# A delta-rule recurrence feeding a soft mixture of experts: keys taken ahead, norms on GpSimd, output products in pairs

## The chip, the cores and the metric

One core of a Trainium2 chip runs the whole program in one launch. The metric is the device time of one execution in microseconds (us). The core has five instruction streams: TensorE (PE in the profile) multiplies matrices out of the on-chip memory SBUF into the accumulator banks PSUM; VectorE (DVE) and ScalarE (ACT) work element by element and empty PSUM; GpSimd (POOL) works element by element on SBUF and issues some transfers; SyncE (SP) only issues transfers (DMAs).

## The reference

For each of 4 batches and 8 heads a state of 48 x 48 is carried over 768 steps:

```python
k_n = k / (np.linalg.norm(k, axis=-1, keepdims=True) + 1e-06)
for t in range(S):
    y[:, :, t] = np.einsum('bhd,bhde->bhe', q[:, :, t], state)
    v_old = np.einsum('bhde,bhd->bhe', state, kt)
    state = state + bt[..., None] * np.einsum('bhd,bhe->bhde', kt, vt - v_old)
```

The outputs y, laid out as 3072 rows of 384, are the x of a soft mixture of 8 experts with 4 slots each:

```python
logits = x @ phi
d = softmax over rows of logits;  slot_input = d.T @ x
slot_out[e] = np.maximum(slot_input[e] @ w1[e], 0.0) @ w2[e]     # 384 -> 1024 -> 384
c = softmax over slots of logits; result = c @ slot_out
```

Everything is float32.

## The kernel before

**Chunks and groups.** The 768 steps are cut into 12 chunks of 64 (`n`), and two chunks make a group (`g`, 6 of them). Inside a chunk the recurrence is turned into matrix products, for which a triangular system has to be inverted. The inversion is done for a whole group at once on VectorE.

**Loads.** `load_kv` loads a chunk of keys or values in two halves of three DMAs each, `load_q` a chunk of queries in two halves of one DMA each. Nearly all are issued by SP. `beta` is loaded by 16 small DMAs on GpSimd's queue. The identity matrix, needed by every transposition, is built on GpSimd (`ident`).

**Key and query products.** `turn(n, a, j)` transposes keys (`trk`, a = 0) or queries (`trq`, a = 1) on PE and copies them out of PSUM (`evTk`, `evTq`). `gram(n, j, part)` multiplies a chunk's keys with its keys (part 0, `...k`), its keys with its queries (part 1, `...q`), or both in one product of twice the width. The key part is copied out by ACT (`evP`, `evR` for the inversion, `evB`), the query part is masked on VectorE (`mskA`). Before the change only group 0 has the two parts apart.

**Inversion** (`invert(g)`). `spread` transposes blocks of the key products on VectorE; it needs the `evP` and `evR` copies of both chunks. From the diagonal, the squared lengths of the keys, the norms and factors are made (`ssq`, then `ln` and `sq` on ACT, then `rec`, `quo`, `nrm`, `nsq`, `inv`, `gm` on VectorE), each on a tile of 128 x 32. `nT` transposes the norms for the scaling of the values (`vs`, on GpSimd from group 1 on). `diag` and `scale` prepare the system. Then come 31 pairs `col`/`sub` (15 for group 0, which is halved and put together on PE by `z`, `v` and `mrg`), each pair depending on the one before. `back` transposes back; behind it `tw` (ACT, and GpSimd for one half from group 1 on) and `j` with `evJ` finish the group on TensorE and ACT.

**Step** (`step(n)`). Chunk after chunk: `ks` (keys by state) and `r` (values less that, VectorE), `tr` with `evW`, `fix` with `evU`, `s` with `evS` (the new state), `qs` (queries by state) and the part `au`, which is mixed into the next chunk's `tr`. `try`, `lg`, `trd`, `trL`, `sl`, `trE` with their copies and the VectorE steps `max`, `emx`, `esb`, `esm`, `enr`, `acc` are the routing of two chunks into the slots.

**Experts and output.** `first` (`fst`), `turnh` (`trh`), `second` (`snd`) are the experts; their weights are loaded into places of the SBUF that earlier stages have left free, and into places of the first weights once those are used. `put(d)` sums the halves (`sum`, `so`) and makes the output products `om`, which ACT and VectorE copy (`evo`) and SP or GpSimd store (`st`).

**Order.** The kernel lists its operations and then emits them in the order of a written-out string (`ORDER`), a permutation of that list; each engine runs its own operations in that order, one after the other. `BANKS` gives the PSUM bank of each product, and `GATES` holds a load of expert weights back until a given product has run. A planner outside the kernel, with fixed costs per operation, made the three strings.

Of the kernel before, what the change touches and what calls it, by code (L numbers as in the profile page):

```python
# [12 lines left out]
ALU = mybir.AluOpType  # L13
# [1 line left out]
PSUM = bass.MemoryType.PSUM  # L15

ORDER = (
    "#*##%x#,#&#0#+#3#$#2#-#%#)#'#(#E#G#D#=#F#6#>$K#?#7#4#8#.#C#@$d#A#O#<#B#H#P#9$e#:#V#I$C#;$G$D#/#Q$H$E"
    "#R$g#U$|#J$F%y#S#N$I#K#L$J#M#T#5#W&Q$r$h$s$i#X$L#Y#Z#[#]#^#d#_$f%z#`&0$?#a#b%{#c$;$@#e#f$A#g$<$M#h#i"
    "$N#j$Y#k&1#l#m#n$t$Z#o$=#p$u$B'}$v#q$>#r$j#s$w$O#t$z&l#u$P#v#1${$k$[#w$x#x$l&P$y#y$]#z&2$Q$p#{$^#|$R"  # L20
    "&3&R$m#}$S'~$q$b$_#~$`$#$$$T$c$W&k$%$a$X$n&S$&&T$o$'$U$V&_&U$}&`$)$($~$-'%$*%#%$%%%&%'%(%-%)(#%*$+%,"
    "$.%+%.%/%0%1%2%3%4$/%5$,%6$2%7%8$1%9%:%;%<%=%>%?$3$0%@$7&#%A$5%B$6%C%|%D&$$4&y%E(Q&%$8%F%}%~%G&z%H&&"
    "$9%I(R$:&a%J&'&V%K&b&*%L&W&c%M&+(s%N&,(t&X%O&g%P&d&(%Q&]%R&Y&o&)&^&e)0&-(S%S&f&4)/%T&.&h&j&/%U&Z%V&["
    "%W&p&9&5&i%X&6&:%Y%Z&;&7*A%[&8%]%^%_%`&>&H%a&<%b*B&K&?%c&=%d&B&I%e&@%f&C%g%h&w&D%i&m%j&A%k&x%l&E%m&n"
    "($(q&F&q&G(%()%t&u(r&r&{(*&s&t)E%u&v&|*t&}%o%p&~%w'&%v(;%r*u%n&J%q'''$'((&')'*'#'+%s','-'2'.*C'/(w'1"
    "(')%(((x(.+:'0)&'3'4(++9'5'6'7(u'8(9'9(8':)#';(v'<(:)$*v'='>(/)='?(,(2'@(-)3'A(3(0'B)4+Q'C(4(>'D+R(<"
# [99 lines left out]
def kernel(  # L126
# [249 lines left out]
    def invert(g):  # L376
# [5 lines left out]
        def spread():  # L382
# [6 lines left out]
        ACTO("ln%d" % g, 32, lambda: S_.activation(A(n0), A(n0), ACT.Ln), more=20, r=[n0], w=[n0])  # L389
        ACTO("sq%d" % g, 32, lambda: S_.activation(A(n0), A(n0), ACT.Exp, scale=0.5), more=20, r=[n0], w=[n0])  # L390
        DVE("rec%d" % g, 32, lambda: V.reciprocal(A(qq), A(n0)), more=165, r=[n0], w=[qq])
        DVE("quo%d" % g, 32, lambda: V.tensor_tensor(A(qq), dg(lb), A(qq), op=ALU.mult), r=[lb], w=[qq])
        DVE("nrm%d" % g, 32, lambda: V.scalar_tensor_tensor(A(nrm), A(n0), 2e-6, A(qq), op0=ALU.add, op1=ALU.add),
            more=55, r=[n0, qq], w=[nrm])
        DVE("nsq%d" % g, 32, lambda: V.scalar_tensor_tensor(A(gm), A(nrm), 0.25, A(nrm), op0=ALU.mult, op1=ALU.mult),
            more=55, r=[nrm], w=[gm])
        DVE("inv%d" % g, 32, lambda: V.reciprocal(A(gm), A(gm)), more=165, w=[gm])
        DVE("gm%d" % g, 32, lambda: V.tensor_tensor(A(gm), A(cbb)[:, 32 * g:32 * g + 32], A(gm), op=ALU.mult),
            r=[cbb], w=[gm])
        DVE("diag%d" % g, 32, lambda: V.tensor_copy(dg(tt), A(gm)), r=[gm], w=[tt])  # L400

        def blk(t):
# [397 lines left out]
    def mkrd():  # L800
# [1 line left out]
        V.reciprocal(A(sS)[:, 3:4], A(sS)[:, 2:3])  # L802
    DVE("rd", 0, mkrd, more=190, r=[prd], w=[(sS, 2)])

    hrb = [Buf(Yr[0], F), Buf(Yr[0] + F, F)]
    hTb = [Buf(Yr[0] + 2 * F, F), Buf(Yr[0] + 3 * F, F)]
    HF, W2 = F // 2, 2 * Dm
    late = [Vr[0], Vr[1], Sbd[0].addr, Sbd[0].addr + W2, KQr[0], KQr[0] + W2, Kr[0], BBr[1], Vr[2],
            Sbd[1].addr, Sbd[1].addr + W2] + [KQr[0] + W2 * x for x in (2, 3, 4)]
    late += Rr + [Ur[0], TWr[1], TWr[1] + W2, AAr[0], Ur[1], AAr[0] + W2, BBr[2]]  # L810
    late += [w1b[e, kk].addr for e in range(3) for kk in range(NKT)]

    def load_w2(qq):
        for u in range(4):
# [47 lines left out]
    obs = [Buf(w1b[e, kk].addr + Dm * x, Dm) for e in range(3, 7) for kk in range(NKT) for x in H2]  # L862

    def second(qq, u, d):
        def prod():
# [8 lines left out]
    def put(d):  # L874
# [6 lines left out]
        DVE("so%d" % d, HC, lambda: V.tensor_scalar(  # L881
            A(so[d]), F1(p4)[:, 0:HC], A(sS)[:, 3:4], None, op0=ALU.mult), r=[p4, (sS, 2)], w=[so[d]])
        for m in range(NG):
            for j in H2:
                po, ob = pl.ps(), obs.pop(0)

                def om(m=m, j=j, po=po):
                    for c in H2:
                        r = slice(64 * c + 32 * j, 64 * c + 32 * j + 32)
                        for e in H2:  # L890
                            a = HD * e + C * m
                            x = HC * (1 - e)
                            mm(F1(po)[ha(c), x:x + HC], A(cT)[r, a:a + C], A(so[d])[r],  # L893
                               tile_position=(64 * c + 32 * j, 64 * c))
                PE("om%d.%d.%d" % (d, m, j), 500, om, rec=16, r=[cT, so[d]], w=[po])
                (DVE if j else ACTO)("evo%d.%d.%d" % (d, m, j), Dm, lambda po=po, ob=ob, j=j: (  # L896
                    V.tensor_copy if j else S_.copy)(A(ob), F1(po)[:, 0:Dm]), r=[po], w=[ob])
                byp = j and m % 2

                def st(j=j, m=m, ob=ob, byp=byp):  # L900
# [33 lines left out]
```

## Time and profile before

| | |
|---|---|
| median of 3 runs | 312.4 us (310.45 to 313.92) |
| profiled execution | 314.56 us, its span 312.8 us |
| TensorE, VectorE, ScalarE, GpSimd busy | 248.1, 212.5, 172.3, 98.4 us |
| mean granted TensorE clock | 0.896 of full speed |
| moved by DMA | 45.11 MB |

The profile is one execution. PE stands for matmuls, PEld for its weight loads, DVE for VectorE, ACT for ScalarE, POOL for GpSimd, SP for SyncE; an engine with a q behind it is its queue of issues. In a timeline row stand the start and the length in us, the engine, the line, the instruction, its output and input and, in brackets, how long the engine had been idle before it and what ended that. In a group row stand the count, the busy time and the mean length in ns. A row of a stretch gives its ends, its length, the busy time of each engine shown with its count of instructions, the granted clock, the DMA share and GB/s. L179 is the line of the helper for ACT's copies, so it holds most of them.

### The profile page before, as it was taken

The numbers are of one execution on the slowest core, as the hardware profiler recorded it, in microseconds if no ns is written. First come the engines' busy times: TensorE is split into PE (matmuls) and PEld (weight loads), VectorE is DVE, ScalarE is ACT, GpSimd is POOL, SyncE is SP. The second block draws the span as 40 slices with busy tenths as digits, with TensorE's granted clock in tenths as the row PEclk, the third lists the DMA queues.
The fourth block names the chain that finished last, engine by engine and source line by source line (L and its number), as shares of the span: only waits on it lengthen the run. The fifth ranks groups of instructions, "written<-read, shape, count | busy, mean of one in ns | idle before, by whom it ended". The sixth has DMA issues, their size and how long they took to land.

```text
span 312.8 us, 14219 instructions
## 1 busy us (share of the span) xinstructions
PE 248.1 (79%) x6168; PEld 199.2 (64%) x6168; DVE 212.5 (68%) x581; ACT 172.3 (55%) x417; POOL 98.4 (31%) x215
## 2 busy tenths in 40 slices
PE   0746965698899789798975887979879698999990
PEld 0644755697787676687854776777758585247770
DVE  3347868974979889999899998997983145010160
ACT  1453471358687858779874768836458454111340
POOL 9820004305058700594006009854403000000031
PEclk9975675559999999999999998979999799899995
DMA  8997990025655444403963153785899579492477
GB/s 110 130 125 106 133 127 5 6 46 86 106 102 81 76 81 70 82 9 55 109 179 54 36 114 99 239 256 145 290 364 332 195 229 355 175 375 77 153 224 231
DMA packets 90734, 45.11 MB, mean 144 GB/s; under 512 B 78480, under 2 KB 83216, under 8 KB 90672
## 3 DMA queue, kind: packets, MB, share of 16 engines
q1 hardware_dynamic: 87632, 42.53, 59.0%
q0 software_dynamic: 896, 1.28, 1.7%
q8 instruction: 48, 0.79, 1.1%
q10 hardware_dynamic: 2144, 0.39, 1.0%
q14 instruction: 14, 0.11, 0.2%
HBM read 39.47 MB, written 4.72 MB: 141 GB/s over the span
## 4 chain that ended last, share of the span: by engine, by line
PE 53%; DVE 18%; ACT 9%; issue 9%; DMA 4%; SPq 3%; POOL 1%; POOLq 0%; ACTq 0%; DVEq 0%
ACT sb L179 9%; PE pb L347 6%; PE pb L328 5%; PE pb L589 5%; PE pb L572 4%; PE pb L829 4%; PE pb L868 4%; PE pb L560 4%; DVE sb L426 4%; DVE sb L421 3%; PE pb L496 3%; PE pb L893 3%; PE pb L603 3%; PE pb L470 2%; DVE sb L384 2%
## 5 line engine op out<-in xcount | busy, mean ns | idle before, releaser
L179 ACT ACTIVATE sb<-pb 128x384 f32<-128x384 f32 (+5 forms) x252 | 111.3, 465 | 54.6 <-PE pb L328 12.9
L532 POOL TENSOR_SCALAR sb<-sb 128x48 f32<-128x48 f32 x160 | 57.7, 387 | 42.9 <-issue 17.5
L421 DVE TENSOR_TENSOR sb<-sb 128x31 f32<-128x31 f32 (+15 forms) x155 | 53.9, 348 | 4.3
L426 DVE TENSOR_TENSOR sb<-sb 128x31 f32<-128x31 f32 (+15 forms) x155 | 53.2, 343 | 4.3
L179 ACT ACTIVATE sb<-pb,sb 128x256 f32<-128x256 f32 (+1 forms) x96 | 39.9, 451 | 28.9 <-PE pb L347 13.4
L328 PE MATMUL pb<-sb 128*128 128x128 f32 x192 | 33.5, 320 | 20.4 <-DMA sb<-in_k_dram 13.0
L328 PEld LDWEIGHTS pb<-sb 128*128 128x128 f32 x192 | 25.0, 163 | 25.2 <-issue 14.8
L485 POOL TENSOR_SCALAR sb<-sb 128x512 f32<-128x512 f32 x10 | 16.6, 1664 | 66.7 <-DVE sb L448 66.7
L347 PE MATMUL pb<-sb 48*64 48x128 f32 (+1 forms) x896 | 29.8, 280 | 4.4 <-DVE sb L366 2.6
L572 PE MATMUL pb<-sb 64*64 64x48 f32 x768 | 28.9, 228 | 4.3 <-DVE sb L562 1.7
L572 PEld LDWEIGHTS pb<-sb 64*64 64x64 f32 x768 | 26.9, 144 | 6.5 <-DVE sb L562 1.7
L347 PEld LDWEIGHTS pb<-sb 48*64 48x64 f32 x896 | 24.3, 149 | 8.0 <-ACT sb L179 3.1
L516 PE MATMUL pb<-sb 64*64 64x48 f32 x768 | 27.7, 222 | 1.4 <-issue 1.4
L589 PE MATMUL pb<-sb 64*64 64x96 f32 x384 | 23.8, 263 | 4.0 <-issue 2.5
L516 PEld LDWEIGHTS pb<-sb 64*64 64x64 f32 x768 | 25.1, 136 | 1.7 <-issue 1.7
L366 DVE TENSOR_TENSOR sb<-pb,sb 128x512 f32<-128x512 f32 x24 | 16.5, 688 | 12.8 <-ACT sb L179 9.4
L902 POOL DMA_DIRECT2D out_dram<-sb x6 | 4.5, 743 | 64.8 <-DVE sb L896 64.8
L589 PEld LDWEIGHTS pb<-sb 64*64 64x64 f32 x384 | 19.3, 145 | 6.4 <-issue 3.1
L560 PE MATMUL pb<-sb 128*64 128x96 f32 x352 | 20.1, 257 | 1.9 <-ACT sb L179 1.7
L622 PE MATMUL pb<-sb 128*64 128x96 f32 x352 | 18.9, 250 | 1.9 <-ACT sb L179 1.4
L496 PE MATMUL pb<-sb 64*64 64x64 f32 x384 | 15.8, 240 | 5.1 <-issue 2.8
L560 PEld LDWEIGHTS pb<-sb 128*64 128x64 f32 x352 | 15.9, 141 | 6.1 <-ACT sb L179 4.6
(114 smaller groups left out, 334.9 us busy)
## 6 DMA issues: line engine op xcount, KB each, us to landing
sb<-in_moe_w_dram SPq DMA_DIRECT2D x24, 512.0 KB, 5.2
sb<-in_moe_w_dram SPq DMA_DIRECT2D x32, 384.0 KB, 5.4
sb<-in_q_dram SPq DMA_DIRECT2D x24, 192.0 KB, 4.7
out_dram<-sb SPq DMA_DIRECT2D x18, 192.0 KB, 2.5
sb<-in_v_dram SPq DMA_DIRECT2D x24, 96.0 KB, 3.4
sb<-in_v_dram SPq DMA_DIRECT2D x48, 48.0 KB, 3.4
sb<-in_k_dram SPq DMA_DIRECT2D x22, 96.0 KB, 3.9
sb<-in_k_dram SPq DMA_DIRECT2D x44, 48.0 KB, 3.6
```

Source lines behind the costliest of these rows:

```text
L179: S_.activation(o, i, ACT.Copy, **kw)
L328: nc.tensor.transpose(F1(ps)[:, P * h:P * h + P], A(src)[:, x:x + P], ident())
L347: mm(A(ps)[ha(e), i, P * h:P * h + P].rearrange("p (a t) -> p a t", a=2)[:, pr[0]:pr[-1] + 1], x[hd(i), j, h, e], y[hd(i), j, h, e, pr[0]: ...
L421: V.tensor_tensor(p(), v3(tt)[:, j:j + 1, 0:m].broadcast_to(sh), v3(lb)[:, j:j + 1, j + 1:32].rearrange("p x i -> p i x").broadcast_to(sh) ...
L426: V.tensor_tensor(t, t, p(), op=ALU.subtract)
L496: mm(F1(pj)[ha(e), C * h:C * h + C], A(bb)[ha(e), b:b + C], A(lb)[ha(e), b:b + C])
L516: mm(F1(pY[n, j])[ha(1 - e), D * x:D * x + D], A(AA[n])[ha(e), a:a + C], A(UB[n])[ha(e), c:c + D], start=n == 0 and x == 0)
L532: G_.tensor_scalar(y, y, A(nb)[:, c:c + 1], 0.5, op0=ALU.mult, op1=ALU.mult)
L560: mm(bank(pK)[ha(e), j, 2 * D * h:2 * D * h + 2 * D], t4(n, 0)[:, j, 2 * b + h, e], bd()[:, j, b, h, e])
L572: mm(bank(pU[b])[ha(e), j, y:y + D], A(TW[g])[ha(e), a:a + C], A(R)[ha(e), c:c + D], start=x == 4 * b and j == 0)
L589: mm(bank(pU[b])[ha(e), :, y:y + D], A(BBb[g])[ha(e), a:a + C], A(U)[ha(e)].rearrange("p (j x d) -> p x j d", j=2, d=D)[:, x], start=False)
L622: mm(F1(pY[n, j])[ha(1 - e), 2 * D * h:2 * D * h + 2 * D], t4(n, 1)[:, j, h, e], bd()[:, j, h // 2, h % 2, e], start=h == 0)
```

## The change

There are four parts. Group 1 makes its key products apart from its query products, as group 0 does. The keys of chunks 0 to 3 are loaded first, then queries and values; beta's loads now stand ahead of the identity on GpSimd. In groups 1 to 5 the norms and factors are made by GpSimd and ACT (an inverse square root and an inverse from logarithm and exponential, each refined by one step), so VectorE keeps only `nT`, `diag` and `scale` of this part. The two output products of a chunk pair become one operation that writes two PSUM banks. All three strings are new, and with them the order of everything else; places of the expert weights move as well.

```diff
-        DVE("ssq%d" % g, 32, lambda: V.tensor_scalar(A(n0), dg(lb), 1e-30, None, op0=ALU.max), r=[lb], w=[n0])
...
+        if g:
+            t_ = lambda o, x, y: G_.tensor_tensor(A(o), A(x), A(y), op=ALU.mult)
+            lin = lambda o, x, a, b: G_.tensor_scalar(A(o), A(x), a, b, op0=ALU.mult, op1=ALU.add)
+            def root():
+                t_(gm, qq, qq)
+                t_(gm, gm, n0)
+                lin(gm, gm, -0.5, 1.5)
+                t_(qq, qq, gm)
+                t_(nrm, n0, qq)
+                lin(nrm, nrm, 2.0, 2e-6)
+            def inverse():
+                t_(gm, nrm, n0)
+                lin(gm, gm, -2.0, 4.0)
+                t_(n0, n0, gm)
+                t_(n0, n0, n0)
+                G_.tensor_tensor(A(gm), A(cbb)[:, 32 * g:32 * g + 32], A(n0), op=ALU.mult)
+            POOL("ssq%d" % g, 200, lambda: G_.tensor_scalar(A(n0), dg(lb), 1e-30, None, op0=ALU.max), r=[lb], w=[n0])
+            act("ln%d" % g, gm, n0, ACT.Ln, 1.0)
+            act("sq%d" % g, qq, gm, ACT.Exp, -0.5)
+            POOL("root%d" % g, 1000, root, r=[n0], w=[qq, gm, nrm])
+            act("lm%d" % g, gm, nrm, ACT.Ln, 1.0)
+            act("iv%d" % g, n0, gm, ACT.Exp, -1.0)
+            POOL("ivs%d" % g, 850, inverse, r=[nrm, cbb], w=[n0, gm])
+        else:
...
@@ get
-                if g:
+                if g > 1:
                     turn(n, 1, j)
                     gram(n, j)
                 else:
                     gram(n, j, 0)
         invert(g)
-        for n in H2 if not g else ():
+        for n in (2 * g, 2 * g + 1) if g < 2 else ():
@@ expert weights
-    late += [w1b[e, kk].addr for e in range(3) for kk in range(NKT)]
+    late += [w1b[e, kk].addr for e in range(2) for kk in range(NKT)][:32 - len(late)]
@@ put
+            po = pl.ps(2)
+            def om(m=m, po=po):
+                for e in H2:
+                    a = HD * e + C * m
+                    x = HC * (1 - e)
+                    for j in H2:
+                        for c in H2:
+                            r = slice(64 * c + 32 * j, 64 * c + 32 * j + 32)
+                            mm(A(po)[ha(c), j, x:x + HC], A(cT)[r, a:a + C], A(so[d])[r], tile_position=(64 * c + 32 * j, 64 * c))
+            PE("om%d.%d" % (d, m), 830, om, rec=32, r=[cT, so[d]], w=[(po, 0), (po, 1)])
             for j in H2:
-                po, ob = pl.ps(), obs.pop(0)
-       ...
-                PE("om%d.%d.%d" % (d, m, j), 500, om, rec=16, r=[cT, so[d]], w=[po])
+                ob = obs.pop(0)
```

The strings, read as sequences, at the places that the prediction speaks of:

```
SP before:   v0.0 k0.0 q1.1 k1.0 q1.0 k2.0 q0.0 k3.0 k3.1 q3.1 v0.1 q0.1 k4.1 k2.1 ...
SP after:    phi k0.0 k2.0 k1.0 k2.1 k3.0 k3.1 q0.0 q0.1 q1.0 q1.1 v0.0 v0.1 v1.0 v1.1 q2.0 ...
             (k0.1 and k1.1 by ACT's queue in both)
POOL after:  beta ident maskA zeroS0 zeroS1 zeroT0 zeroT1 ssq1 root1 vs2 ivs1 zeroT2 vs3 tw3.1 tw2.1
             zeroT3 ssq2 root2 ivs2 vs4 vs5 tw5.1 zeroT4 tw4.1 ssq3 root3 ivs3 vs6 ...
PE before:   ... trk5.1 trk5.0 s1.1 ks2.0 gram5.0 ks2.1 gram5.1 j3 j2 ...
PE after:    ... ks1.0 s0.1 tr1.0 qs1.0 fix1.0 j2 s1.0 ks1.1 j3 qs1.1 trk5.1 tr1.1 trk5.0 trq6.0
             fix1.1 try0.1 trq6.1 s1.1 gram5.1 gram5.0 ks2.1 ks2.0 ...
DVE before:  ... backT1 r2.0 r2.1 mskA5.0 spread2 ssq2 mskA5.1 rec2 quo2 nrm2 nsq2 nT2 inv2 gm2 scale2 diag2 col2.0
DVE after:   ... col1.27 r1.0 sub1.27 mskA4.1 ... backT1 r1.1 mskA5.1 mskA5.0 spread2 r2.1 r2.0 nT2 scale2 diag2 col2.0
ACT after:   ... evTk2.0 evB3.0 evP3.0 evR3.0.0 evR3.0.1 evP2.1 evTq0.1 evTq0.0 ln0 evTq1.1 sq0 ...
```

More of the change, by code (lines that the diff above doesn't have):

```diff
@@ L60 @@
+    "1$2G1L2F1L1L"
 )
@@ L387, in invert @@
         v3 = lambda t: A(t).rearrange("p (r c) -> p r c", c=32)
-        DVE("ssq%d" % g, 32, lambda: V.tensor_scalar(A(n0), dg(lb), 1e-30, None, op0=ALU.max), r=[lb], w=[n0])
[L389 to L399, printed above, removed]
+        if g:
[14 more added lines that the diff above has]
+                G_.tensor_tensor(A(gm), A(cbb)[:, 32 * g:32 * g + 32], A(n0), op=ALU.mult)
+            act = lambda name, o, x, f, c: ACTO(name, 32, lambda: S_.activation(A(o), A(x), f, scale=c), more=20, r=[x], w=[o])
+            POOL("ssq%d" % g, 200, lambda: G_.tensor_scalar(A(n0), dg(lb), 1e-30, None, op0=ALU.max), r=[lb], w=[n0])
[6 more added lines that the diff above has]
+        else:
+            DVE("ssq%d" % g, 32, lambda: V.tensor_scalar(A(n0), dg(lb), 1e-30, None, op0=ALU.max), r=[lb], w=[n0])
+            ACTO("ln%d" % g, 32, lambda: S_.activation(A(n0), A(n0), ACT.Ln), more=20, r=[n0], w=[n0])
+            ACTO("sq%d" % g, 32, lambda: S_.activation(A(n0), A(n0), ACT.Exp, scale=0.5), more=20, r=[n0], w=[n0])
+            DVE("rec%d" % g, 32, lambda: V.reciprocal(A(qq), A(n0)), more=165, r=[n0], w=[qq])
+            DVE("quo%d" % g, 32, lambda: V.tensor_tensor(A(qq), dg(lb), A(qq), op=ALU.mult), r=[lb], w=[qq])
+            DVE("nrm%d" % g, 32, lambda: V.scalar_tensor_tensor(A(nrm), A(n0), 2e-6, A(qq), op0=ALU.add, op1=ALU.add),
+                more=55, r=[n0, qq], w=[nrm])
+            DVE("nsq%d" % g, 32, lambda: V.scalar_tensor_tensor(A(gm), A(nrm), 0.25, A(nrm), op0=ALU.mult, op1=ALU.mult),
+                more=55, r=[nrm], w=[gm])
+            DVE("inv%d" % g, 32, lambda: V.reciprocal(A(gm), A(gm)), more=165, w=[gm])
+            DVE("gm%d" % g, 32, lambda: V.tensor_tensor(A(gm), A(cbb)[:, 32 * g:32 * g + 32], A(gm), op=ALU.mult),
+                r=[cbb], w=[gm])
@@ L861 @@
     so = [Buf(rt[0] + HC * x, HC) for x in H2]
-    obs = [Buf(w1b[e, kk].addr + Dm * x, Dm) for e in range(3, 7) for kk in range(NKT) for x in H2]
+    obs = [Buf(w1b[e, kk].addr + Dm * x, Dm) for e, kk in [(7, 0), (7, 1), (3, 2)] + [(e, kk) for e in (4, 5, 6) for kk in range(NKT)]
+           for x in H2]
     def second(qq, u, d):
```

95 lines of the change are left out of this document (43 added, 52 removed).

## The prediction

> **What bounds the kernel now.** I read the page's chain first, then the stretches between landmarks on VectorE (DVE), whose order is fixed by the written-out list. The chain's shares:
>
> ```profile
> PE 53%; DVE 18%; ACT 9%; issue 9%; DMA 4%; SPq 3%; POOL 1%; POOLq 0%; ACTq 0%; DVEq 0%
> ```
>
> The chain keeps stepping onto TensorE (PE), yet the middle is paced by DVE. The next view gives each stretch, its length, DVE's busy time with count, TensorE's granted clock, DMA share and GB/s. I cut it at starts of DVE operations: `rec0` 25.09, `col0.0` 28.76, `backT0` 44.22, `col1.0` 53.62, `backT1` 85.38, `col2.0` 96.98, `backT2` 126.06, `col3.0` 134.21, `backT5` 232.25, and the copy `evslb` 265.49, after which the experts start.
>
> ```profile
> 25.09:28.76 3.67, 3.39 (x12) 0.50 0.77 123
> 28.76:44.22 15.46, 11.73 (x39) 0.72 0.91 119
> 44.22:53.62 9.40, 8.63 (x14) 0.50 0.38 45
> 53.62:85.38 31.76, 23.78 (x69) 0.74 0.37 58
> 85.38:96.98 11.60, 9.28 (x16) 1.00 0.52 93
> 96.98:126.06 29.08, 25.72 (x77) 1.00 0.50 78
> 126.06:134.21 8.15, 7.91 (x15) 1.00 0.45 77
> 134.21:232.25 98.04, 89.27 (x250) 0.97 0.57 146
> 232.25:265.49 33.24, 13.03 (x47) 0.94 0.81 282
> ```
>
> From 96.98 to 232.25 DVE is busy 122.9 of 135.3 us: there its own work sets the pace. Before that it also waits (23.78 of 31.76), mostly in one place:
>
> ```profile
> 74.68 0.70 DVE L366 TENSOR_TENSOR sb<-pb,sb 128x512 f32<-128x512 f32 x1 [6.06 <-ACT sb L179]
> ```
>
> After 232.25 DVE is idle most of the time, and PE finishes chunks 10 and 11, routing, experts and output. So I follow DVE to `backT5`, then add the two tail stretches.
>
> **Start: keys ahead.** A chunk of q, k or v is 0.39 MB. Landings in before:
>
> ```profile
> 12.84 1.06 PE L328 MATMUL pb<-sb 128*128 128x128 f32 x8 [0.22 <-DMA sb<-in_k_dram]
> ...
> 26.58 1.94 PE L328 MATMUL pb<-sb 128*128 128x128 f32 x8 [2.53 <-DMA sb<-in_q_dram]
> ```
>
> Counting issues ahead of each, 1.28 MB had landed at the first and 2.95 MB at the second: 122 KB/us. In the new order keys 0 to 3 with phi and beta are 1.72 MB, estimated at 16.4 us; q0 at 19.7, q1 at 22.9. `gram1.1k` now stands behind `trk3.0`, so it runs at about 17.5, and `spread0` starts near 20 (19.5 before). ScalarE (ACT) then holds `ln0` behind the copy of q0 and `sq0` behind one of q1 (22.9, a transposition and two copies): `rec0` at about 25, as before. I take no gain; with 125 KB/us and no landing lag it is 3 us, and 1.5 us of loss if ACT's queue drains late. Beta's 16 issues (8.9 us, row below) now precede the identity, so first transposes start near 10.8; the wait for chunk 3's keys covers that.
>
> Behind `rec0`: `mskA0.0` and `mskA1.1` move ahead of `col0.0`, 0.62 us each (0.70 in the row of L366, and starts overlap by 0.08): `col0.0` at 30.0. The next stretch loses some 3.0 us of waits and two masks and gains `mskA1.0` 0.62, `spread1` 1.85 and `nT1` 0.13: 13.85, `backT0` at 43.85. Then `spread1` (1.8), group 1's norm (1.9) and its ACT wait (0.6) are gone and `mskA2.1` is added: 5.8 instead of 9.4. `col1.0` starts at **49.7** (53.6). This needs `ivs1` by 48; POOL runs it behind `vs2`, which ends near 46. Cover gone, each microsecond costs one.
>
> **Norms off DVE.** Seven small instructions per group leave DVE in groups 1 to 5. What they cost now, from reciprocal to the scaling behind them:
>
> ```profile
> 93.90 0.36 DVE L391 RECIPROCAL sb<-sb 128x32 f32<-128x32 f32 x1
> ...
> 95.62 1.23 DVE L411 TENSOR_TENSOR sb<-sb 128x1024 f32<-128x1024 f32 x1
> ```
>
> That is 1.7 us, 8.5 in five groups if nothing waits. In exchange POOL gets 12 instructions (`ssq` 1, `root` 6, `ivs` 5) and ACT two more. No POOL row shows 32-element arithmetic. The nearest:
>
> ```profile
> L532 POOL TENSOR_SCALAR sb<-sb 128x48 f32<-128x48 f32 x160 | 57.7, 387 | 42.9 <-issue 17.5 <-PE pb L328 13.2 <-DMA sb<-in_v_dram 7.6
> L485 POOL TENSOR_SCALAR sb<-sb 128x512 f32<-128x512 f32 x10 | 16.6, 1664 | 66.7 <-DVE sb L448 66.7
> L271 POOL DMA_DIRECT2D sb<-in_beta_dram x16 | 8.9, 566 | 0.6 <-DMA sb<-in_beta_dram 0.5
> ...
> L282 POOL TENSOR_SCALAR_AFFINE_SELECT sb<-sb 32x64 f32<-32x64 f32 x8 | 1.9, 232 | 0.4
> ```
>
> 387 ns is the upper end, 232 the lower row; an unrowed two-input form could go below, say 0.17, or above. I take 0.3: 3.6 us, plus 1.1 for four ACT steps and hand-overs, 4.7 us of chain. The Trainium skill, GPSIMD Engine Reference, section "Performance versus the Vector engine", speaks against the move: two-input elementwise work takes GpSimd about twice DVE's time. No run here shows such an instruction; twice DVE's 0.2 us would make the chain some 1.2 us longer than I take.
>
> The chain is hidden where `spread` stands well ahead of `back`: group 1, and nearly groups 4 and 5 (4.9 and 4.5 us of DVE work against a chain of some 5 to 5.5; 0.7 and 0.5 us show). In groups 2 and 3 `spread` stands behind `backT`, and DVE waits.
>
> **Group 1 to 2: a new wait.** `mrg0` moves to behind `col1.15`, 63 us. So `tr0.0` starts near 65 (62 before). PE here runs at half clock:
>
> ```profile
> 45.00:69.00 24.00, 17.48 (x657) 16.23 (x658) 21.69 (x52) 8.73 (x21) 6.76 (x17) 0.50 0.19 25
> ```
>
> (PE, PE loads, DVE, ACT, POOL, clock.) With half speed to about 70 as before, `ks1.0` ends near 75; `r1.0` behind `col1.27` would be ready at 72.3, so DVE waits 2.7. The stretch to `backT1` is 31.76 less 6.06 less `r1.1` 0.47 plus 2.7: `backT1` at 77.6 (85.4), 7.8 early.
>
> That gain is lost. In before's PE order `gram5.0` and `gram5.1` precede `j3 j2`. In the new one `j2`, which needs `backT1`, comes first, then `s1.0 ks1.1 j3 qs1.1 trk5.1 tr1.1 trk5.0 trq6.0 fix1.1 try0.1 trq6.1 s1.1 gram5.1 gram5.0`, and `spread2` needs `gram5.0`. PE at full clock, 72 to 100 us (busy, mean ns):
>
> ```profile
> L572 PE MATMUL pb<-sb 64*64 64x48 f32 x128 | 4.5, 218 | 1.6 <-DVE sb L562 0.8 <-issue 0.5 <-ACT sb L179 0.3
> L347 PE MATMUL pb<-sb 48*64 48x128 f32 x128 | 4.2, 272 | 0.2 <-ACT sb L179 0.2
> L328 PE MATMUL pb<-sb 128*128 128x128 f32 x28 | 4.2, 283 | 0.0
> L589 PE MATMUL pb<-sb 64*64 64x96 f32 x64 | 3.6, 245 | 0.1
> L560 PE MATMUL pb<-sb 128*64 128x96 f32 x64 | 3.5, 252 | 0.4 <-ACT sb L179 0.4
> L622 PE MATMUL pb<-sb 128*64 128x96 f32 x60 | 3.1, 250 | 0.0
> L496 PE MATMUL pb<-sb 64*64 64x64 f32 x64 | 2.0, 217 | 0.0
> L603 PE MATMUL pb<-sb 64*48 64x48 f32 x96 | 2.0, 210 | 0.9 <-issue 0.9
> ```
>
> Per operation: `j` (32 matmuls of L496) 1.0, `s` 0.67, `ks` 0.88, `qs` 0.83, `tr` 1.15, `fix` 0.9, a gram 1.05, a transposition of four 0.6, `try` 0.5. Two `j`, two `s`, one `ks`, `qs`, `tr`, `fix`, `try`, four transpositions, two grams: 12.1, with hand-overs 12.5. Behind it five copies of `gram5.0` and the rest, ACT:
>
> ```profile
> L179 ACT ACTIVATE sb<-pb,sb 128x256 f32<-128x256 f32 x4 | 1.7, 479 | 0.7 <-PE pb L347 0.7
> L179 ACT ACTIVATE sb<-pb 32x256 f32<-32x256 f32 x4 | 1.5, 385 | 0.1
> ```
>
> 2.0 us. So from `backT1` at 77.6: 2.0 itself, 14.6 to `spread2`, 2.0 that, 4.7 chain, 1.4 scaling and diagonal: `col2.0` at **102.3**, 5.3 late. DVE idles about 15 us in between.
>
> **Group 3.** Stretch `col2.0` to `backT2` loses six routing and mask operations (2.3): `backT2` 129.1. Behind it POOL has `tw5.1`, `zeroT4`, `tw4.1` (1.66, 0.95, 1.66) before `ssq3`, and ACT has `evW4.0` and `eex0` before `lm3`: `ssq3` 4.6 us behind the transposition, `root3` done at 7.2, `ivs3` at 9.3, `col3.0` at 10.7 (6.2 before): `col3.0` at 141.8, 7.6 late.
>
> **Groups 4 and 5** give back 4.5. Their norms are worth 3.0 (group 4's stand between other starts and cost less), 1.2 of it exposed. Two waits for PE sit where the new order has moved the waiting operation on by several columns:
>
> ```profile
> 213.40 0.61 DVE L693 SCALAR_TENSOR_TENSOR sb<-sb,pb 128x384 f32<-128x384 f32 x1 [1.86 <-PE pb L687]
> ...
> 228.51 0.29 DVE L668 TENSOR_REDUCE sb<-pb 128x1 f32<-128x128 f32 x1 [0.83 <-PE pb L657]
> ```
>
> They go: 2.7. `r10.0`, `emx3`, `esb3` move behind `backT5`, `esm2` and `enr2` ahead of it, 0.9 each way. `backT5` at **235.4**, 3.1 late; the two waits, if they come back elsewhere, cost their 2.7.
>
> **Tail.** Behind `backT5` PE now has `qs10.0` and `qs10.1` (1.7), less `trE2`: +1.0. The 24 output products become 12 of twice the size with the same matmuls. The last ones and the last stores:
>
> ```profile
> 297.50 6.82 PE L893 MATMUL pb<-sb 32*64 32x192 f32 x128
> ```
>
> ```profile
> out_dram<-sb SPq DMA_DIRECT2D x18, 192.0 KB, 2.5
> ...
> out_dram<-sb POOLq DMA_DIRECT2D x6, 192.0 KB, 4.3
> ```
>
> Both halves of the last product are now copied side by side on ACT and DVE (0.5), and the last store goes by SP, 2.5 against 4.3 us to landing, of which I count 1.5: -2.0, bounds -0.5 and -4. Weights of the experts change place, with fewer loads behind the first products; PE did not wait for them before, so nothing.
>
> **Sum:** +3.1 +1.0 -2.0 = **+2.1 us**. The profiled execution took 314.56 (span 312.8 and 1.76 around it), so 316.7 on its scale; on the median of 312.4 it is **314.5**. One per cent, 3.1 us, is about what a measurement of this kernel can tell from no change.
>
> **Rivals.**
> - *Keys ahead do bring the start forward.* The forecast has that part of the change do nothing. If landings have no lag, `rec0` comes near 22 and everything behind it 3 to 4 early: 310.8. For it: keys no longer share the queue with q and v. Against: `ln0` and `sq0` wait for q0 and q1 on ACT. 0.17.
> - *Cheap GpSimd steps.* At 0.17 us each the chain is 1.6 shorter in groups 2 and 3, and hidden in 4 and 5: -4.3, 310.2. For: 232 ns for 64 elements. Against: 387 for 48. 0.18.
> - *Slower: PE stays at half clock.* Place: `tr0.0` to `gram4.1`, ahead of `ks1.0`. It decides from 72.3 us on, when `r1.0` waits. Two `tr` (1.8 each at half clock), two `fix`, two transpositions of four, `s`, a gram and `ks` come to 14.5 us there at half clock and 7.5 at full, so `ks1.0` ends at 79.5, 4.5 later, and everything behind the strict order follows: 319. For: 0.50 for 24 us with PE busy. Against: transpositions now stand between the small products. 0.25. The Trainium skill, "TensorE: Matmul & The Clock Gate", section "The HAM clock gate", has the gate open after about 3.4 us of sustained work. The row of 45 to 69 disagrees (17.48 of 24 busy at 0.50); by that rule `ks1.0` would end at 72.5 and the time be 312.
> - *Output products overlap.* With its two halves in two banks the product could run at half of its time, until copies bound it (7 pairs of 0.65 against 6.8): -2.2, 312.3. For: nothing in a trace yet. 0.10. The Trainium skill, "TensorEngine Tiling (Array Packing)", section "Restrictions and Gotchas", says that different row tiles can't use one bank at once, which would be this rival.
>
> **How the numbers follow.** Forecast 0.30. Errors of the steps add to about 6 us; the ends of start (-3, +1.5), steps (-4.3, +3) and clock (-2.5, +4.5) give 306 to 322. Faster by over 1% (under 309.3): half of the two early rivals and a part of the forecast's lower side, 0.28. Within: 0.34. Slower (over 315.5): the clock rival and the forecast's upper side, 0.38.
>
> **What would show it.** `rec0` near 25; `col1.0` near 50; a DVE wait of over 10 us ahead of `spread2`, ended by ACT; POOL's small steps near 0.3 us; a wait ahead of `scale3`; last stores from SP. The forecast is wrong if `gram5.0` isn't what `spread2` waits for, if the start moves by more than 3 us, or if the clock opens before 60.

## The result, and the profile after

The changed kernel takes 330.4 us (median of four, 327.4 to 331.1), the one before 313.2 (median of four, 310.5 to 316.3, three of them from ahead of the prediction): ratio 1.056, 95% interval 1.045 to 1.067. It is slower, and outside the range that was forecast. Each ratio sets those executions of a kernel that lie within 1.5% of its fastest against those of the kernel before that were timed beside it, while a median takes them all, so kernels of different experiments are best compared by their ratios. The profiled execution took 331.1 us, its span 329.4: it is the longest of the four.

The chain, as it was read first of before:

```profile
PE 38%; DVE 22%; POOL 12%; issue 8%; SPq 6%; ACT 6%; DMA 4%; POOLq 0%; DVEq 0%; ACTq 0%
```

GpSimd (POOL) had 1% of it and has 12% now. The same stretches, cut at the same operations (start to end, length, DVE busy with count, granted clock, DMA share, GB/s):

```profile
27.28:31.75 4.47, 4.33 (x14) 0.77 0.84 118
31.75:45.87 14.12, 13.19 (x40) 0.50 1.07 124
45.87:51.42 5.55, 5.55 (x6) 0.50 0.54 46
51.42:78.99 27.57, 23.61 (x68) 0.71 0.36 50
78.99:103.42 24.43, 8.45 (x11) 0.93 0.44 76
103.42:129.57 26.15, 24.03 (x69) 0.98 0.49 74
129.57:143.34 13.77, 8.91 (x16) 0.78 0.26 46
143.34:249.92 106.58, 89.05 (x237) 0.89 0.50 128
249.92:284.54 34.62, 13.16 (x45) 0.90 0.82 268
284.54:329.40 44.86, 10.58 (x19) 0.89 0.72 237
```

In the table stand the starts before, as forecast (where the text gives only a length, added up), after, and in e1, the first experiment below.

| operation | before | forecast | after | e1 |
|---|---|---|---|---|
| `col1.0` | 53.6 | 49.7 | 51.4 | 50.7 |
| `backT1` | 85.4 | 77.6 | 79.0 | 78.6 |
| `spread2` | 91.1 | 94.2 | 94.9 | 94.5 |
| `col2.0` | 97.0 | 102.3 | 103.4 | 103.1 |
| `backT2` | 126.1 | 129.1 | 129.6 | 129.2 |
| `col3.0` | 134.2 | 141.8 | 143.3 | 143.0 |
| `backT5` | 232.3 | 235.4 | 249.9 | 239.7 |
| `evslb` | 265.5 | 269.6 | 284.5 | 273.8 |
| end of span | 312.8 | 314.9 | 329.4 | 316.9 |

Down to `col3.0` the forecast holds within 2 us. Then a stretch that took 98.04 us takes 106.58, with DVE's own work unchanged (89.05 against 89.27): it waits. Which instructions wait, first in DVE's timeline, then in TensorE's (PE):

```profile
200.69 0.61 DVE L718 SCALAR_TENSOR_TENSOR sb<-sb,pb 128x384 f32<-128x384 f32 x1 [3.90 <-PE pb L712]
239.93 0.56 DVE L587 TENSOR_TENSOR sb<-sb,pb 128x384 f32<-128x384 f32 x1 [5.51 <-PE pb L585]
```

```profile
192.94 0.26 PE L597 MATMUL pb<-sb 64*64 64x48 f32 x2 [2.99 <-POOL sb L510]
235.09 0.35 PE L597 MATMUL pb<-sb 64*64 64x48 f32 x2 [6.69 <-POOL sb L510]
```

L597 is `tr`, L510 the scaling `tw`. GpSimd's timeline says why `tw` was late:

```profile
177.93 1.60 POOL L510 TENSOR_SCALAR sb<-sb 128x512 f32<-128x512 f32 x1
179.52 11.82 POOL L557 TENSOR_SCALAR sb<-sb 128x48 f32<-128x48 f32 x32
191.31 1.58 POOL L510 TENSOR_SCALAR sb<-sb 128x512 f32<-128x512 f32 x1
...
217.81 2.65 POOL L510 TENSOR_SCALAR sb<-sb 128x512 f32<-128x512 f32 x1
220.44 12.86 POOL L557 TENSOR_SCALAR sb<-sb 128x48 f32<-128x48 f32 x32
233.28 1.75 POOL L510 TENSOR_SCALAR sb<-sb 128x512 f32<-128x512 f32 x1
```

`tw6.1` runs, then `vs8` and `vs9` (32 small scalings, 11.82 us), and only then `tw7.1`, for which `tr7` waits; the same with `tw8.1`, `vs10`, `vs11` and `tw9.1`. Before, `tw7.1` stood ahead of `vs8`, and `tw9.1` ahead of `vs10`.

### The profile page after: what moved, and what is told of

It is laid out like the page before. It is cut to its first block, busy times and chain, and to the rows that moved or that the text cites. A ratio compares the mean times of both kernels' runs of the same rounds, so it can differ in the third digit from the quotient of the medians.

```text
span 329.4 us, 14515 instructions
## 1 busy us (share of the span) xinstructions
PE 255.1 (77%) x6296; PEld 205.3 (62%) x6296; DVE 208.8 (63%) x546; ACT 173.7 (53%) x427; POOL 114.3 (35%) x275
## 4 chain that ended last, share of the span: by engine, by line
PE 38%; DVE 22%; POOL 12%; issue 8%; SPq 6%; ACT 6%; DMA 4%; POOLq 0%; DVEq 0%; ACTq 0%
POOL sb L557 7%; DVE sb L451 5%; DVE sb L446 5%; ACT sb L177 5%; PE pb L856 4%; PE pb L896 3%; SPq L297 3%; PE pb L597 3%; PE pb L647 3%; DVE sb L382 3%; DVE sb L364 3%; PE pb L521 3%; PE pb L585 3%; PE pb L326 3%; PE pb L495 2%
## 5 line engine op out<-in xcount | busy, mean ns | idle before, releaser
L326 PE MATMUL pb<-sb 128*128 128x128 f32 x192 | 35.0, 328 | 11.7 <-POOL sb masks.py:199 11.4
L345 PE MATMUL pb<-sb 48*64 48x64 f32 (+1 forms) x1024 | 35.2, 289 | 9.4 <-ACT sb L177 5.4
L345 PEld LDWEIGHTS pb<-sb 48*64 48x64 f32 x1024 | 29.2, 167 | 14.6 <-ACT sb L177 8.5
L597 PE MATMUL pb<-sb 64*64 64x48 f32 x768 | 28.8, 231 | 11.5 <-POOL sb L510 9.9
L597 PEld LDWEIGHTS pb<-sb 64*64 64x64 f32 x768 | 26.8, 146 | 13.6 <-POOL sb L510 10.6
L541 PE MATMUL pb<-sb 64*64 64x48 f32 x768 | 29.9, 232 | 1.7 <-issue 1.7
L510 POOL TENSOR_SCALAR sb<-sb 128x512 f32<-128x512 f32 x10 | 17.0, 1708 | 34.6 <-DVE sb L473 17.6
L587 DVE TENSOR_TENSOR sb<-sb,pb 128x384 f32<-128x384 f32 x22 | 12.2, 554 | 24.9 <-PE pb L585 13.8
L541 PEld LDWEIGHTS pb<-sb 64*64 64x64 f32 x768 | 27.0, 145 | 0.6 <-issue 0.5
L405 POOL TENSOR_SCALAR sb<-sb 128x32 f32<-128x32 f32 x5 | 1.7, 349 | 69.0 <-DVE sb L382 69.0
L585 PE MATMUL pb<-sb 128*64 128x96 f32 x352 | 21.6, 273 | 4.9 <-ACT sb L177 4.8
L647 PE MATMUL pb<-sb 128*64 128x96 f32 x352 | 20.1, 262 | 4.6 <-DVE sb L587 2.0
L585 PEld LDWEIGHTS pb<-sb 128*64 128x64 f32 x352 | 17.7, 152 | 8.0 <-ACT sb L177 7.3
L614 PE MATMUL pb<-sb 64*64 64x96 f32 x384 | 22.1, 257 | 0.4 <-ACT sb L177 0.4
```

The source lines that it names most:

```text
L326: nc.tensor.transpose(F1(ps)[:, P * h:P * h + P], A(src)[:, x:x + P], ident())
L345: mm(A(ps)[ha(e), i, P * h:P * h + P].rearrange("p (a t) -> p a t", a=2)[:, pr[0]:pr[-1] + 1], x[hd(i), j, h, e], y[hd(i), j, h, e, pr[0]: ...
L541: mm(F1(pY[n, j])[ha(1 - e), D * x:D * x + D], A(AA[n])[ha(e), a:a + C], A(UB[n])[ha(e), c:c + D], start=n == 0 and x == 0)
L585: mm(bank(pK)[ha(e), j, 2 * D * h:2 * D * h + 2 * D], t4(n, 0)[:, j, 2 * b + h, e], bd()[:, j, b, h, e])
L597: mm(bank(pU[b])[ha(e), j, y:y + D], A(TW[g])[ha(e), a:a + C], A(R)[ha(e), c:c + D], start=x == 4 * b and j == 0)
L614: mm(bank(pU[b])[ha(e), :, y:y + D], A(BBb[g])[ha(e), a:a + C], A(U)[ha(e)].rearrange("p (j x d) -> p x j d", j=2, d=D)[:, x], start=False)
```

## The experiments

**e1: GpSimd's order.**

```diff
 GpSimd: ... tw6.1
+        tw7.1
         vs8 vs9
-        tw7.1
         zeroT5 ssq5 root5 ivs5 tw8.1
+        tw9.1
         vs10 vs11
-        tw9.1
```

> The changed kernel with one thing moved: on GpSimd tw7.1 goes ahead of vs8 and vs9, and tw9.1 ahead of vs10 and vs11. Theory A (GpSimd's order is the loss of the stretch col3.0 to backT5): tr7 and tr9 wait for these two scalings, which stand behind 12 us of vs each; the DVE waits of 3.90 (acc2) and 5.51 (r9.1) go, backT5 comes 8 to 12 us earlier (238 to 242 instead of 249.9), and the time is 319 to 323, ratio to before about 1.025. Rival B (the stretch is lost to the norm chain and to PE's own order): backT5 moves by less than 3 us, time 328 to 331.

Measured: 321.8 us, ratio 1.035 (1.025 to 1.046); profiled 318.6, the shortest of its four executions. `backT5` starts at 239.66, 10.3 earlier. TensorE's waits from 143 to 250 us, first line of the list of after (for what; us, times, longest) and then of e1, and e1's stretches:

```profile
PE pb L597 <- POOL sb L510: 9.9, 3, 6.7
```

```profile
PE pb L597 <- DVE sb L587: 3.2, 3, 1.9
```

```profile
142.96:239.66 96.70, 88.83 (x238) 0.95 0.53 142
239.66:273.81 34.15, 13.15 (x45) 0.95 0.78 265
273.81:316.90 43.09, 10.57 (x19) 0.96 0.74 250
```

The waits of 3.90 and 5.51 are gone, and the stretch takes 96.70: theory A holds, B falls. Between the two profiles, the two moved scalings are worth 9.9 us of it. After's profile is of its longest execution and e1's of its shortest, so this is the larger figure: by the ratios the move is worth 2.1 of the 5.6 percent, some 6.5 us. The 3.5 percent that e1 still lies above before (0.7 were forecast) are only in part accounted for below.

**e2 and e6: PE's order behind `backT1`.** Of the forecast's loss behind `backT1`, is the order the cause? In e2:

```diff
-PE: tr1.0 qs1.0 fix1.0 j2 s1.0 ks1.1 j3 qs1.1 trk5.1 tr1.1 trk5.0 trq6.0 fix1.1 try0.1 trq6.1 s1.1 gram5.1 gram5.0
+PE: tr1.0 qs1.0 ks1.1 fix1.0 s1.0 tr1.1 trk5.1 qs1.1 trk5.0 fix1.1 gram5.0 gram5.1 s1.1 j2 j3
```

> The changed kernel with the order of PE and ACT between tr1.0 and ks2.0 changed: the second half of step 1 and gram5 run ahead of j2 and j3, as in the kernel before. Theory C (PE's order costs VectorE its idle time ahead of spread2): spread2 near 89.5 to 90.5 instead of 94.9 (keys of chunk 5 land near 84, then transpositions, copies, product, copies), col2.0 4 to 5 us earlier, time 325 to 328 (ratio about 1.04), since what follows is untouched. Rival: spread2 is early, but r2.0 and r2.1 or the scaling are then waited for and col2.0 moves by less than 2 us; or tr7 and tr9 wait for GpSimd anyway and the time stays at 330.

Measured: 340.5 us, ratio 1.100 (1.093 to 1.108), worse than any theory. `spread2` came at 92.61, 2.3 earlier and not 5. The keys of chunk 5 landed at 83.69, and their transpositions followed at once, in PE's timeline:

```profile
83.91 0.66 PE L326 MATMUL pb<-sb 128*128 128x128 f32 x4
```

With PE's order out of the way, then, the load is what comes next. From there to `spread2` it took 8.7 us, where before took 6.6: the transpositions behind had to wait for ACT's copies of the earlier ones.

And it went wrong behind that, by the experiment's own order. On ACT `sq2` was left behind copies of later transpositions. The two steps, which should follow each other at once, in ACT's timeline:

```profile
96.39 0.24 ACT L404 ACTIVATE sb<-sb 128x32 f32<-128x32 f32 x1
...
100.95 0.23 ACT L404 ACTIVATE sb<-sb 128x32 f32<-128x32 f32 x1
```

Two later steps, `iv2` and `lm2`, stood behind the copy of chunk 6's keys, which SP had issued only behind queries at 100.7. TensorE waited for these keys until 107.70, ACT ran the two steps at 109.32, and the columns of group 2 began at 112.93, 9.5 later than in after. First PE's wait, then what VectorE waited for:

```profile
107.70 1.09 PE L326 MATMUL pb<-sb 128*128 128x128 f32 x4 [6.03 <-DMA sb<-in_k_dram]
```

```profile
103.15 0.21 DVE L438 STREAM_TRANSPOSE sb<-sb 128x32 f32<-128x32 f32 x1 [4.43 <-POOL sb L388]
111.52 1.23 DVE L436 TENSOR_TENSOR sb<-sb 128x1024 f32<-128x1024 f32 x1 [8.16 <-POOL sb L403]
```

So the chain, six hand-overs between three engines, depends on a place in each of their queues, and SP's queue of loads can hold it too. e6 put ACT's steps first, issued chunk 6's keys earlier and kept e1's order on GpSimd:

> The kernel of e1 with PE, ACT and SP between tr1.0 and ks2.0 in another order: as in e2, but with ln2, sq2, lm2 and iv2 on ACT ahead of the copies that wait for j2, j3 and the later transpositions, and k6 issued ahead of q8.1. Theory C (PE's order holds spread2 back): spread2 at 91 to 93 (94.5 in e1; the keys of chunk 5 land near 84 to 86 and cap it), col2.0 at 98 to 100 (103), and 3 to 4 us kept to the end: 315 to 318, ratio about 1.025. Rival (other orders behind it take the gain back, such as the routing steps among the columns of group 2): col2.0 early, backT2 within 1 us of e1, time as e1, ratio 1.035.

Its four executions took 323.1 to 334.8 us, further apart than the effect looked for, and the profile is of the longest: it decides nothing, nor does its `spread2` at 96.29 speak for an earlier one.

**e3 and e7: the norms back on VectorE**, in after's order (e3) and in e1's (e7):

```diff
-        if g:
+        if g > NG:      # the form of before for every group
```

> The changed kernel with the norms and factors of groups 1 to 5 back on VectorE in the form of before (nine instructions, two on ACT), each in the place that its GpSimd form had. Theory D (the GpSimd chain costs more than it saves): the waits of 1.09, 2.00, 1.43, 0.66 and 0.45 us ahead of nT and scale go, and 1.7 us of VectorE work per group come back, about 3 of it where VectorE idles: col2.0 and col3.0 each about 2 earlier, groups 1, 4 and 5 each 0 to 1.5 later, time 327 to 331. Rival: the chain hides the more where PE is late, and the seven instructions on VectorE cost their full 8.5: time 333 to 338.

> The kernel of e1 with the norms of groups 1 to 5 on VectorE as in e3. Theory D (with GpSimd's order mended, the norm chain is what remains): waits ahead of nT and scale in groups 2 and 3 go and 1 to 2 us each are kept, time 316 to 319, ratio 1.02 to 1.03. Rival (the chain only fills time that PE leaves idle anyway): ratio 1.035 to 1.045, the seven instructions per group come back in groups 1, 4 and 5.

Measured: e3 328.4, ratio 1.061 (1.053 to 1.069); e7 322.1, ratio 1.037 (1.027 to 1.047). Neither differs from its partner (1.056 and 1.035). That is a sum of gains and losses, in the profiles:

- Group 2 gains by the norms on VectorE. From `backT1` to `col2.0` e3 takes 22.8 against 24.4 in after, e7 22.3 against 24.5 in e1.
- Group 3 gains hardly anything. From `backT2` to `col3.0` it is 13.1 against 13.8 in e3, and 13.8 against 13.7 in e7.
- Group 1 loses what it had hidden in e7, where `backT1` comes at 81.27 against e1's 78.59. In e3 it doesn't.
- Groups 4 and 5 lose 1.9 in e7, from `col3.0` to `backT5`, all of it in VectorE's own work (90.76 against 88.83 in e1):

```profile
145.16:243.78 98.62, 90.76 (x251) 0.93 0.52 139
```

In the whole time it makes no difference in these orders on which engine the norms are: theory D falls for the sum. In groups 4 and 5, where e1's order has no late scaling, the norms on GpSimd bring 1.9 us.

**e8: the norms alone.** The kernel before, in its own order, with only the norms moved:

```diff
-DVE:  rec quo nrm nsq inv gm (groups 1 to 5)
+POOL: ssq root ivs, ACT: ln sq lm iv, each where the reciprocal stood
```

> The kernel before with only the norms of groups 1 to 5 moved to GpSimd and ACT, each step in the place of the reciprocal that it replaces, all else in the order of before. By the prediction's reading the chain of 4.7 us replaces 1.7 us of VectorE work: groups 2 and 3 lose 2 to 4 us each (backT1 to col2.0 13 to 15 us instead of 11.6, backT2 to col3.0 10 to 13 instead of 8.15), group 4 gains 0 to 1.7, group 1 changes by -1 to +2; group 5 has tw8.1, tw9.1 and vs8, vs9 ahead of it in GpSimd's queue and may lose 5 to 10. Time 320 to 328, ratio 1.03 to 1.05. Rival (norms on GpSimd are nearly free, 0.3 us each beside idle VectorE): ratio 0.99 to 1.01.

Measured: 324.0, ratio 1.042 (1.033 to 1.052). Its stretches `backT0` to `col1.0`, to `backT1`, to `col2.0`, to `backT2`, to `col3.0`:

```profile
43.62:55.93 12.31, 7.29 (x6) 0.51 0.26 33
55.93:82.37 26.44, 24.04 (x68) 0.84 0.44 67
82.37:97.48 15.11, 7.98 (x9) 0.92 0.42 75
97.48:126.63 29.15, 25.92 (x78) 0.98 0.48 77
126.63:138.38 11.75, 6.34 (x8) 0.90 0.29 53
```

Against before: +2.9, -5.3, +3.5, +0.1, +3.6. Groups 2 and 3 lose as the forecast's working has it, and group 3's columns 2.6 more, to a routing step that comes late. Group 4's chain is hidden (`backT3` to `backT4` 30.84 against 30.85), group 5's columns begin 3.6 later behind `backT4` (12.0 against 8.4), of which all but 0.8 is made up by `backT5`: far from the 5 to 10 feared. So this part of the change, put into that order, costs some 4%; the -5.3 goes with a clock that came to full earlier, at 64.2 against 70.3 in before, of which more at b3.

**e4 and e4_again: the output alone**, the changed `put` with its order in the kernel before:

> The kernel before with the output part of the changed one alone: joined products, their order, banks and stores. By the prediction 2.0 us less (bounds 0.5 and 4): 310.5 on 312.5, ratio 0.994. Rival (products in two banks overlap): 4 us less, ratio 0.987, with the products' busy time near half. If the tail is set by copies and stores: no change.

> The kernel of e4 once more, with more rounds, on the chip of this call: 1 to 2 us less than before, ratio 0.993 to 0.998. Rival: no difference, 0.998 to 1.002.

Measured: 0.997 (0.992 to 1.002), then with more executions 0.994 (0.989 to 1.000): 1 to 2 us less, at the edge of what these runs can tell. The profiles agree: the stretch from `evslb` to the end takes 44.3 and 45.9 us, against 47.31 in before.

**e9: step chain early.** If neither PE's order nor the norms hold `spread2`, is it the start of step 0? On e1, with ACT, DVE, SP and the PSUM banks to match:

```diff
-PE: z0 trq4.0 z1 trq4.1 v1 gram4.0 v0 trq5.0 j1 j0 tr0.0 tr0.1 ...
+PE: z0 z1 v0 v1 j0 tr0.1 tr0.0 trk4.1 trq5.1 j1 fix0.0 trq4.1 trq4.0 s0.0 gram4.1 gram4.0 ...
```

> The kernel of e1 with the work between z0 and ks2.0 in the order of before: z0 z1 v0 v1 follow each other, mrg0 stands behind column 8 of group 1 and mrg1 behind column 12 (11 and 15 in e1), tr0 follows, gram4 and the transpositions of chunks 4 and 5 come behind, and step 1 and gram5 stand ahead of j2 and j3. Theory E (from tr0.0 on, the step chain on PE sets spread2, not VectorE: in the changed kernel tr0.0 starts at 68.1 and spread2 26.8 later, in the one before at 62.0 and 29.1 later): tr0.0 near 62 to 64, spread2 at 89 to 92 (94.5 in e1), col2.0 at 97 to 99 (103), and 3 to 5 us kept to backT2; time 315 to 319. Rival (spread2 is held by PE's order behind backT1 or by the load of chunk 5's keys): spread2 moves by less than 2 us. What is kept behind backT2 is open: groups 3 and 4 may take it back.

Measured: 334.4, ratio 1.064 (1.057 to 1.070). `tr0` came at 62.4, as meant, but `spread2` at 93.04, only 1.5 earlier; what followed lost it many times over. Theory E falls. The transpositions of chunk 5's keys again stood last, waiting for the load:

```profile
86.47 1.07 PE L326 MATMUL pb<-sb 128*128 128x128 f32 x8 [1.13 <-DMA sb<-in_k_dram]
```

These keys are loaded into the place of chunk 0's, which `s0.1` reads. In after SP issues the load as soon as `s0.1` has ended. In e9 `s0.1` ended no later, but SP still had the queries of chunk 7 and values to issue, and came to these keys at 79.89. For each kernel, after first, the end of `s0.1` on PE and the issue on SP:

```profile
75.79 0.57 PE L628 MATMUL pb<-sb 64*48 64x48 f32 x32
```

```profile
76.22 0.61 SPq L293 DMA_DIRECT2D sb<-in_k_dram  x1
```

```profile
75.03 0.57 PE L628 MATMUL pb<-sb 64*48 64x48 f32 x32
```

```profile
79.89 0.61 SPq L293 DMA_DIRECT2D sb<-in_k_dram  x1
```

The keys had landed at 83.5 in after, 83.7 in e2 and 86.3 in e9. Their first transposition ran at 84.5 in before, 85.4 in after (where no wait for the load is shown, and TensorE is busy with other work until then), 83.9 in e2, 86.5 in e9. As an estimate, with a landing at 83.5 and the 6.6 us from the first transposition to `spread2` in before, no order of TensorE's or VectorE's alone brings `spread2` below 90. Neither keys in a place of their own nor an earlier issue on SP was tried.

**e10: identity first**, on e1:

```diff
-GpSimd: beta ident maskA ...
+GpSimd: ident beta maskA ...
```

> The kernel of e1 with the identity matrix built ahead of beta's loads on GpSimd. The prediction held the identity (done at 11.4) to be covered by the wait for the keys of chunk 3. Theory F (it is not: everything on PE behind it starts late): first transposition at 7 to 9 instead of 11.4, spread0 at 19.5 to 20.5 instead of 22.0, rec0 at 25 to 26.5 instead of 27.3, col1.0 1 to 2 earlier, time 1 us less than e1 (ratio 1.03) since spread2 is set elsewhere. Rival (the keys of chunk 3 and the copies on ACT set spread0): spread0 within 0.5 us of 22.0, no change of time.

Measured: 320.1, ratio 1.018 (1.010 to 1.027) against e1's 1.035 (1.025 to 1.046): the intervals meet, so whether the kernel got faster is open. The first transposition starts at 5.17 instead of e1's 11.49, `spread0` at 21.32 (22.07), `rec0` at 25.80 (26.55). In PE's timeline:

```profile
5.17 1.09 PE L326 MATMUL pb<-sb 128*128 128x128 f32 x4 [5.17 <-DMA sb<-in_k_dram]
```

`spread2` starts at 94.48, in e1 at 94.54: six microseconds at the first instruction are 0.06 there. The profile is of e10's longest execution (324.6).

**b1 and b3: versions.** b1 has e4's operations in an order worked out anew, from the durations of the profiles:

> The kernel before with the joined output products (e4) and another order of the same operations on every engine, in which each operation that is waited for stands ahead of those that are not, by the durations that the profiles show; nothing in the operations changes. If the orders are what costs and not the operations: spread2 3 to 8 us earlier than in before, 298 to 306 us, ratio 0.96 to 0.985. Rival (the middle is VectorE's own work, and the start the loads): 307 to 311, ratio 0.99 to 1.0.

Measured: 335.5, ratio 1.066 (1.058 to 1.074). From `backT2` to `spread4` it took 41.7 us (31.6 in e4), with waits of VectorE of 2.12 us for TensorE and 3.50 for ACT. Our reading, which no run shows: packed so that each operation stands just where its input should be ready, the order has no slack left, and a small lateness is passed on to everything behind.

b3 takes the two parts that had not cost anything: the joined output, and the norms of group 1 alone.

```diff
-        if g:
+        if g == 1:      # on e4; zeroT2 behind ivs1 on GpSimd
```

> The kernel before with the joined output products (e4) and the norms of group 1 alone on GpSimd and ACT, in the places that they had in e8; groups 2 to 5 keep theirs on VectorE. In e8 col1.0 came 2.3 us later than in before, backT1 nevertheless 3.0 earlier, with TensorE's granted clock at full 4 us earlier. If that shift belongs to this order of work: 2 to 3 us less at backT1, of it 2 kept at spread2, and 1 from the output: 308 to 310 on 312, ratio 0.988 to 0.993. Rival (the clock opened earlier in that one execution by chance): col1.0 2 later, backT1 at 85 to 87, ratio 0.997 to 1.005.

Measured over 12 executions: 309.8 us, ratio 0.988 (0.980 to 0.997): faster than before by about 1%, and than the change. It isn't shown to be faster than e4's kernel, whose median beside it is 309.4 over 12 executions (ratio 0.994): that group 1's norms add anything stays open. As in e8, `backT1` came early (82.18), with the clock at full 4 us earlier (PE busy, clock, from 64 us; e4_again first, then b3):

```profile
64.00:66.00 2.00, 2.00 (x23) 0.50 0.00 0
66.00:68.00 2.00, 2.00 (x37) 0.50 0.59 108
```

```profile
64.00:66.00 2.00, 2.00 (x52) 0.99 0.08 13
66.00:68.00 2.00, 2.00 (x47) 1.00 0.59 110
```

In both profiles with group 1's chain on GpSimd in this order (e8, b3) the clock comes to full at 64 us, in all three without it (before, e4, e4_again) behind 68. Five profiles are too few to call it shown, and they pair unlike executions: b3's is of its fastest (304.9), those of e4 and e4_again of their longest (314.0 and 315.2).

## Why the prediction was wrong

- **Start.** Forecast: no gain, `spread0` near 20, `rec0` at 25. Measured 22.0 and 27.3. "The wait for chunk 3's keys covers that" was wrong: in e10 the identity first brought `rec0` 0.75 earlier than in e1. That explains a third of the 2 us; the rest stays open, e1 and after differing by 0.7 here without any change so early. At `spread2` the mistake cost nothing.
- **Group 1.** `col1.0` 1.7 and `backT1` 1.4 later than forecast, by the late start. The 6.06 us wait for a mask is gone, as said.
- **Group 1 to 2.** The new wait was named with its place and size: 14.6 us from the end of `backT1` to `spread2`, measured 14.0, with these waits of DVE for the two masks:

```profile
92.67 0.69 DVE L364 TENSOR_TENSOR sb<-pb,sb 128x512 f32<-128x512 f32 x1 [8.54 <-ACT sb L177]
94.33 0.69 DVE L364 TENSOR_TENSOR sb<-pb,sb 128x512 f32<-128x512 f32 x1 [0.97 <-ACT sb L177]
```

  Its cause, PE's order, was right for this kernel: the keys of chunk 5 had landed at 83.5 and were transposed at 85.4. But they leave little more to gain, as e2 (landing at 83.7, transposed at 83.9) and e9 (TensorE waiting for them) show. The gain of 6.4 us at `backT1` was bounded from the start by a load, into a place that step 0 must give free and at a turn in SP's queue. The forecast's wait of 2.7 for `r1.0` was 1.29.
- **The chain on GpSimd.** Estimated at 4.7 us with 0.3 a step; in group 2:

```profile
96.97 0.33 POOL L405 TENSOR_SCALAR sb<-sb 128x32 f32<-128x32 f32 x1 [10.22 <-DVE sb L382]
...
98.57 0.22 POOL L388 TENSOR_SCALAR sb<-sb 128x32 f32<-128x32 f32 x1
98.87 0.59 POOL L387 TENSOR_TENSOR sb<-sb 128x32 f32<-128x32 f32 x2
...
101.74 0.24 POOL L403 TENSOR_TENSOR sb<-sb 128x32 f32<-128x32 f32 x1
```

  5.0 us, with 0.22 to 0.33 a step: right. The rule of the Trainium skill that was quoted (GPSIMD Engine Reference, "Performance versus the Vector engine", twice VectorE's time) would give 0.4 for a two-input step; two take 0.59 here, 0.3 each, so at this size the trace disagrees.
- **Group 3.** `col3.0` at 141.8 forecast, 143.3 measured, but from `backT2` on 12.7 were forecast and 13.8 taken, and not by the way that was given. `ssq3` was to be held by `tw4.1` ahead of it on GpSimd. `tw4.1` ended at 135.7, and GpSimd then waited for VectorE, where `spread3` (134.59) had stood behind `r4.1`, which waited 1.53 for TensorE. GpSimd's row:

```profile
136.66 0.32 POOL L405 TENSOR_SCALAR sb<-sb 128x32 f32<-128x32 f32 x1 [0.98 <-DVE sb L382]
```

  That the number is near is in part luck.
- **Groups 4 and 5: the step that failed.** They "give back 4.5"; in fact they lost 8.5 (106.58 against 98.04). Of the 13.0 us between forecast and measurement, e1 shows 9.9, as the profiles have it, to be the two scalings behind `vs`. The prediction had walked GpSimd's queue in group 3, where the norms stand, and not in groups 4 and 5, where the new order had put `tw7.1` and `tw9.1` behind the long scalings; the GpSimd string that it quoted ends ahead of these moves, and none of its four rivals held this. In e1 the stretch gives back 1.3 of the 4.5. The missing 3.2 aren't the norms: e7 against e1 has them at 1.9, much as counted (3.0 less exposed waits of 1.2). Nor are they the two waits of TensorE that were to go, for they went. VectorE's busy time fell by only 0.4 against before (88.83 against 89.27) where 3.0 had been counted; why stays open.
- **Tail.** `backT5` to `evslb` +1.4 (+1.0 forecast), experts and output 44.86 against 47.31, -2.4 (-2.0): right.
- **The rivals.** Keys ahead, cheap steps and the slow clock did not happen: the clock was at 1.00 from 67 us. Output products ran a fifth faster: in the last row of the kind 112 took 4.78 us, 0.043 each, where 128 had taken 6.82, 0.053 each, both at a clock of 1.00. Whether they overlapped or the new order did it isn't shown.

## What to carry to other kernels

When an engine with one queue gets new work, go through its whole queue to the end of the kernel and, for every operation that has changed sides with a long one, name who waits: here two scalings of 1.6 us behind 12 us of work that nobody yet needed cost 9.9 of the 16.6 us that the profiled span grew (2.1 of the 5.6 percent by the ratios). The same holds for a queue of loads: in e2 and e9 keys came late because others stood ahead of them on SP. A gain is kept only as far as the next thing that doesn't move with it, so before counting one, look for the load, slot or step that fixes the next start. An order fitted by hand or by one profile's durations is a risk of its own: three of ours lost some 9 us or more where the reasons for them promised a gain.

## What the runs showed of the hardware

In after, each of TensorE's two waits for `tw` (2.99 and 6.69 us) is followed by a lower granted clock. The stretches around them (length, PE busy with count, granted clock), after first, then e1:

```profile
192.00:200.00 8.00, 6.66 (x153) 0.60 0.36 65
...
232.00:240.00 8.00, 4.92 (x100) 0.50 0.23 68
```

```profile
192.00:200.00 8.00, 6.29 (x168) 1.00 0.41 74
...
232.00:240.00 8.00, 6.00 (x134) 1.00 0.86 299
```

With the waits the clock is at 0.60 and 0.50, in e1 it stays at full. e3, which has after's order on GpSimd, shows the same (0.57 from 192 to 200 us, 0.51 from 230 to 237). e7, with e1's order, is at full in the first stretch and at 0.81 in the second, so the second is less clear. What the lower clock costs is within the 9.9 us and hasn't been separated from the waits. The scatter between executions of one kernel goes with the clock too, though the runs don't show which follows which: over 23 executions of before, time and mean granted clock correlate with -0.80, and b3 took 304.9 us at its highest clock, 0.938, and 312.1 at its lowest, 0.895.
